# Lightning attention and a tanh-shrink layer on one core: q and k tiles read as runs of 224 numbers

## The chip, the cores and the metric

The kernel runs on one core of a Trainium2 chip. The core has a matrix engine (PE, with PEld for its weight loads), a vector engine (DVE), ScalarE (ACT), GpSimd (POOL), which here only issues transfers, and SyncE (SP), which issues transfers too. Sixteen DMA engines move the data of all queues. The metric is the device time of one execution in microseconds (us); lower is better.

## What is computed

The input is q, k and v of shape (4, 8, 768, 64) (batch, head, token, head size), a decay lam for each head, and two weight matrices. A decaying linear attention is followed by a two-layer network without bias; all arithmetic is in 32-bit floats (the weights come as 64-bit floats and are rounded on the chip).

```python
for b in range(nb):                       # blocks of 64 tokens
    intra = einsum('bhic,bhjc->bhij', qb, kb) * Dmask
    intra = einsum('bhij,bhjd->bhid', intra, vb)
    inter = einsum('bhid,bhde->bhie', qb * lam_pow, kv_state)
    out[:, :, sl] = intra + inter
    kv_state = lam_block * kv_state + einsum('bhsd,bhse->bhde', kb * rev_pow, vb)
x = out.transpose(0, 2, 1, 3).reshape(3072, 512)
h = x @ w_in                              # 512 x 2048
return (h - tanh(h)) @ w_out              # 2048 x 512
```

## The kernel before

The 768 tokens are cut into six groups of 128 (g = 0 to 5); a group has the four batches, so 512 rows go through the network together. The two matrix products are computed with fewer multiplications, by sums and differences of quarter blocks (seven products in place of eight, for some of them twice nested), so the vector engine adds and subtracts a great deal beside PE. The factors of the weights are made once, written to scratch memory (`factors`, `fine`, `fine_in`), and streamed back from there into a ring of eight tiles `wb` of 256 KB by POOL's queue, one after the other as PE frees them.

Attention needs q and k with the head size on the partitions. For groups 0 and 1, PE transposes natural tiles. For groups 2 to 5 SP loads q and k a second way (`load_blocks`, L143 to L152): a tile `blk` of 128 partitions by 4 by 128 numbers. Partitions 32c to 32c + 31 hold a quarter of a pair of heads (c // 2 chooses the head, c % 2 the half of the head size), and each line of 32 numbers is one token's half. A tile takes 16 transfers, each of 128 runs of 32 numbers (128 bytes). VectorE then transposes each 32 by 32 square (`STREAM_TRANSPOSE`, L335) into qt or kt, one instruction of 512 numbers a partition for each, and multiplies qt by the decay into qd (L346). There are 4 groups x 4 batches x 2 = 32 such tiles; they come from a pool of seven (`late["blk"]`, L1098).

The order of SP's transfers is written out by hand in `load` (L154 to L186), and every transfer of it is kept in program order: for a group, q and k of batches 0, 1, 2, then q of batch 3, natural k and v of batches 0 and 1, k of batch 3, natural k and v of batches 2 and 3 (for group 2 the natural tiles of batches 0 to 2 come first). A transfer waits for the one eight before it on the queue and, if its tile was used before, for the transposes that read the tile. What waits holds up all that is behind it on SP.

Attention of a group is done in pieces during the network's work on the group before it: transposes, scores (PE L362, masked on DVE at L367), state (PE L437, DVE L441 and L443), old state times qd (PE L482), scores times v (PE L501). Batches 2 and 3 are transposed in the midst of the nested second product (`down_twice`, PE L908), batches 0 and 1 near its end and in the first product (`inner_steps`, PE L697, with L686, L688, L714 and L716 taking results from PE's banks). The transposes of DVE are kept in program order; the rest of DVE's order is put together by a scheduler. In `down_twice`, L914 subtracts one quarter from another, which PE's second zw step then reads. The natural k tiles are decayed on ScalarE (L404).

Of the kernel before, what the change touches and what calls it, by code (L numbers as in the profile page):

```python
# [9 lines left out]
F32 = mybir.dt.float32  # L10
# [8 lines left out]
BLK = 128  # L19
# [5 lines left out]
def kernel(  # L25
# [32 lines left out]
    nc = tc.nc  # L58
    B, H, S, D = q.shape
    NTOK, DM = out.shape  # L60
    DFF = moe_w_in.shape[1]
    NP = H // 2
# [62 lines left out]
    def tied(yes, op):  # L125
        return tc.keep_in_program_order(op) if yes else op


    raw, late = {}, {}
    chunks = [(g, b) for g in range(NG) for b in range(B)]  # L130
    at = {"loaded": 0}

# [10 lines left out]
    def load_blocks(g, b, names):  # L143
        for name, src in (("q", q), ("k", k)):
            if name in names:
                x = late["blk"].tile([128, NP, BLK // 32, 32], F32, name=f"{name}_blk", tag="blk")
                for p in range(NP):
                    for c in range(4):
                        blk = src[b, 2 * p + c // 2, ts(g, BLK), ts(c % 2, 32)]
                        tc.keep_in_program_order(  # L150
                            nc.sync.dma_start(out=x[ts(c, 32), p], in_=blk.rearrange("(r t) a -> t r a", t=32)))  # L151
                raw[g, b][name + "b"] = x  # L152

    def load(n):  # L154

        while at["loaded"] < min(n, len(chunks)):
            g, b = chunks[at["loaded"]]
            if g < GB:  # L160
                raw[g, b] = {}
                load_natural(g, b, "qk")
                for x in (b - 1, b) if b % 2 else ():
                    load_natural(g, x, "v")
                at["loaded"] += 1
                continue
            for b in range(B):
                raw[g, b] = {}
            nat = "kv"

            first = (0, 1, 2) if g == GB else ()
            for b in first:
                load_natural(g, b, nat)
            for b in range(B - 1):
                load_blocks(g, b, "qk")
            load_blocks(g, 3, "q")
            for b in (0, 1):
                if b not in first:
                    load_natural(g, b, nat)
            load_blocks(g, 3, "k")  # L180
            for b in (2, 3):
                if b not in first:
                    load_natural(g, b, nat)
            at["loaded"] += B
# [113 lines left out]
    def bank(name, tag, bufs):  # L298
        return psum.tile([128, 512], F32, name=name, tag=tag, bufs=bufs)
# [27 lines left out]
    def att_transpose(g, bs):  # L327
        for b in bs:
            load(g * B + b + 1)
            t = raw[g, b]  # L330
            qt = work.tile([128, NP, BLK], F32, name="qt", tag="qt")
            kt = work.tile([128, NP, BLK], F32, name="kt", tag="kt")
            for dst, x in ((qt, "q"), (kt, "k")):
                if g >= GB:
                    tc.keep_in_program_order(nc.vector.transpose(out=dst.rearrange("d p i -> d (p i)"),  # L335
                                                                 in_=t[x + "b"].rearrange("d p r a -> d (p r a)")))
                else:
                    tp = bank("tp", "att", 4).rearrange("d (p s) -> d p s", p=NP)
                    for p in range(NP):
                        tied(g == 0 or p == 0, nc.tensor.transpose(out=tp[:, p, :], in_=t[x][:, 2 * p:2 * p + 2, :],  # L340
                                                                   identity=ident))
                    tied(g == 0, nc.scalar.activation(dst, tp, AF.Copy))
            qd = None
            if g > 0:
                qd = work.tile([128, NP, BLK], F32, name="qd", tag="qd")
                nc.vector.tensor_tensor(  # L346
                    qd.rearrange("d p (a i) -> d p a i", a=2), qt.rearrange("d p (a i) -> d p a i", a=2),
                    fwd[:, :, None, :].to_broadcast([128, NP, 2, HALF]), op=AL.mult)
            tr[g, b] = (qt, kt, qd)
            if g == 1:  # L350
                att_decay(g, b)
# [37 lines left out]
    def att_decay(g, b):  # L389
        kp = raw[g, b]["k"].rearrange("s (p j) d -> s p j d", j=2)  # L390
        if g > 0:
            nc.vector.tensor_tensor(kp, kp, bwd, op=AL.mult)
            return
        for j in range(2):
            tc.keep_in_program_order(nc.vector.tensor_tensor(
                kp[:, :, j, :], kp[:, :, j, :], whole[j][:, :, BLK - 1:BLK].to_broadcast([128, NP, D]), op=AL.mult))
# [122 lines left out]
    def attention(g):  # L519
        pieces = [[(fn, g, bs) for fn in (att_transpose, att_scores, att_state, att_inter, att_intra)] for bs in ((0, 1), (2, 3))]  # L520
        pieces[1].append((att_sums, g, None))
        return pieces
# [504 lines left out]
    for b in (0, 1):  # L1027
        att_transpose(0, (b,))
        att_decay(0, b)
        att_scores(0, (b,))  # L1030
    att_state(0, (0, 1))
    half = up_plain(0, (11, 21))
    att_transpose(0, (2,))
    att_decay(0, 2)
    weights(1)
# [59 lines left out]
            sums_in((1, 4, 6).index(kt))  # L1095
    first_results()
    early.close()
    late["blk"] = ctx.enter_context(tc.tile_pool(name="blk", bufs=2 * B - 1))  # L1098
    late["pool"] = ctx.enter_context(tc.tile_pool(name="late", bufs=1))


# [165 lines left out]
```

## Time and profile before

| | us |
|---|---|
| three runs | 651.76, 652.22, 656.49 |
| median | 652.22 |
| the profiled execution | 656.83 |
| its span, first to last instruction | 655.1 |

The page's other lines of interest, as shares of the span: the queue of POOL's transfers took 50.4% of the sixteen DMA engines' time for 104.62 MB in 31,792 packets, SP's queue 26.3% for 34.12 MB in 136,224 packets. Where the document shows the order of time of an engine, the columns are start, duration, engine, line, operation, what it writes and reads, and in brackets how long the engine stood idle before it and what released it. In the view of waits, the columns are the total, the number of times and the longest. A group of instructions shows total and mean duration (us, then ns), then the idle time before it.

From the same profiled execution: SP issues a `blk` transfer in 0.43 us (median) and a tile's 16 in 7.6 to 14.8 us; q tiles are transposed in 693 to 712 ns, k tiles in 661 to 714 ns.

### The profile page before, as it was taken

What the parts mean: (1) busy time and instruction counts of PE and PEld (TensorE: products, weight loads), DVE (VectorE), ACT (ScalarE), POOL (GpSimd) and SP (SyncE); (2) the same over time, 40 slices, a digit from 0 to 9 for tenths busy, and PEclk for the clock granted to TensorE, in tenths of its full rate; (3) what the DMA queues carried; (4) which work ended last, traced back from release to release, by engine and by line L of the source; (5) the groups of instructions that cost most, each with busy time, mean ns of one, the idle gap of its engine ahead of it and who ended that gap; (6) DMA issues with size and microseconds to landing.
All of it is one profiled execution on the core that took longest, in us unless ns stands there. A gap on an engine that the chain in (4) does not pass through costs nothing.

```text
span 655.1 us, 16636 instructions
## 1 busy us (share of the span) xinstructions
PE 638.0 (97%) x6440; PEld 586.0 (89%) x6440; DVE 478.5 (73%) x948; ACT 267.5 (41%) x620; POOL 228.4 (35%) x397
## 2 busy tenths in 40 slices
PE   7899999999999999799999999999899999999998
PEld 6788878888888999798899998899898899998997
DVE  4577697776798875669966679988567987467953
ACT  4799585403431422245241246333335342333310
POOL 0000345745533453410355530254320245521251
PEclk9999999999999999899999999999999999999999
DMA  9999998968765998785799985698883377742394
GB/s 212 219 247 237 284 274 295 322 181 244 230 166 140 266 289 235 210 192 121 195 243 275 303 226 153 156 277 247 263 179 99 104 244 226 246 126 68 90 305 150
DMA packets 168238, 139.80 MB, mean 213 GB/s; under 512 B 136864, under 2 KB 138016, under 8 KB 168160
## 3 DMA queue, kind: packets, MB, share of 16 engines
q0 software_dynamic: 31792, 104.62, 50.4%
q1 hardware_dynamic: 136224, 34.12, 26.3%
q8 instruction: 51, 0.84, 0.5%
q14 instruction: 27, 0.22, 0.1%
q10 hardware_dynamic: 144, 0.00, 0.0%
HBM read 111.94 MB, written 26.74 MB: 212 GB/s over the span
## 4 chain that ended last, share of the span: by engine, by line
PE 78%; DVE 8%; DMA 7%; SPq 3%; ACT 2%; issue 1%; DVEq 0%; ACTq 0%
PE y L697 9%; PE plain L851 9%; PE y L908 9%; PE acc L995 7%; PE h L966 7%; PE zw L908 7%; PE z L697 5%; PE y L554 4%; PE y L619 3%; PE zs L619 3%; DMA k_blk<-in_k_dram 3%; PE w L697 2%; PE z L554 2%; SPq L151 2%; DMA q_blk<-in_q_dram 2%; PE op L501 2%
## 5 line engine op out<-in xcount | busy, mean ns | idle before, releaser
L795 POOL DMA_DIRECT2D wb<-fine x133 | 71.6, 539 | 158.8 <-PE plain L851 107.9
L851 PE MATMUL plain<-wb,g 128*128 128x256 f32 x416 | 96.0, 381 | 0.0
L851 PEld LDWEIGHTS plain<-wb,g 128*128 128x128 f32 x416 | 77.5, 190 | 10.4
L966 PE MATMUL h<-xt,w 128*128 128x256 f32 x256 | 57.9, 382 | 1.8 <-DVE w L296 1.8
L798 POOL DMA_DIRECT2D wb<-factors x64 | 34.5, 539 | 70.3 <-PE z L697 47.9
L966 PEld LDWEIGHTS h<-xt,w 128*128 128x128 f32 x256 | 47.7, 190 | 9.0 <-DVE w L296 2.0
L912 ACT ACTIVATE q<-y 128x128 f32<-128x128 f32 x76 | 21.1, 278 | 79.9 <-PE y L908 78.7
L908 PE MATMUL y<-wb,g 128*128 128x128 f32 x336 | 44.8, 278 | 0.0
L688 ACT ACTIVATE g<-y 128x512 f32<-128x512 f32 x24 | 14.3, 597 | 71.5 <-PE y L697 71.5
L792 POOL DMA_DIRECT2D wb<-fine_in x60 | 32.5, 543 | 28.7 <-PE z L697 11.9
L600 ACT ACTIVATE th<-g 128x512 f32<-128x512 f32 x48 | 29.5, 627 | 30.2 <-DVE g L625 30.1
L908 PEld LDWEIGHTS y<-wb,g 128*128 128x128 f32 x336 | 40.7, 192 | 0.7
L404 ACT ACTIVATE k_nat<-k_nat,mask 128x64 f32<-128x64 f32 (+1 forms) x128 | 35.0, 335 | 1.1 <-DMA k_nat<-in_k_dram 1.1
L697 PE MATMUL z<-tt,wb 128*128 128x128 f32 x256 | 32.7, 280 | 0.0
L995 PE MATMUL acc<-wt,g 128*128 128x256 f32 x144 | 32.7, 380 | 0.0
L601 DVE TENSOR_TENSOR g<-g,th 128x512 f32<-128x512 f32 x48 | 32.0, 684 | 0.4
L697 PEld LDWEIGHTS z<-tt,wb 128*128 128x128 f32 x256 | 31.1, 196 | 0.0
L995 PEld LDWEIGHTS acc<-wt,g 128*128 128x128 f32 x144 | 27.3, 190 | 3.7
L619 PE MATMUL y<-xt,w 128*128 128x256 f32 x128 | 30.3, 379 | 0.0
L619 PE MATMUL zs<-xt,ws 128*128 128x256 f32 x128 | 30.2, 379 | 0.0
L908 PE MATMUL zw<-wb,g 128*128 128x128 f32 x224 | 30.2, 278 | 0.0
L292 ACT ACTIVATE r<-raw 128x512 int16<-128x512 uint32 x32 | 25.0, 782 | 7.9 <-DMA raw<-in_moe_w_out_dram 3.5
(233 smaller groups left out, 1475.8 us busy)
## 6 DMA issues: line engine op xcount, KB each, us to landing
wb<-fine POOLq DMA_DIRECT2D x133, 256.0 KB, 3.9
wb<-factors POOLq DMA_DIRECT2D x64, 256.0 KB, 4.5
wb<-fine_in POOLq DMA_DIRECT2D x60, 256.0 KB, 5.1
v_nat<-in_v_dram SPq DMA_DIRECT2D x24, 256.0 KB, 5.2
raw<-in_moe_w_out_dram POOLq DMA_DIRECT2D x12, 512.0 KB, 6.1
k_nat<-in_k_dram SPq DMA_DIRECT2D x20, 256.0 KB, 4.9
fine<-wt POOLq DMA_DIRECT2D x17, 256.0 KB, 3.7
raw<-in_moe_w_in_dram SPq DMA_DIRECT2D x8, 512.0 KB, 6.0
```

The source lines that it names most:

```text
L404: tc.keep_in_program_order(nc.scalar.activation(k_h, k_h, AF.Copy, scale=mask[0:rows, h % 2, h // 2, HALF - 1:HALF]))
L554: nc.tensor.matmul(out=t[:, m, :], lhsT=wt[:, kt, ts(m, 128)], rhs=x[:, kt, :], start=first and m == 0 and kt == 0, stop=kt == 1, skip_gro ...
L601: nc.vector.tensor_tensor(dst(c), src, th, op=AL.subtract)
L619: nc.tensor.matmul(out=t[:, m, :], lhsT=wt[:, kt, ts(m, 128)], rhs=x[:, kt, :], start=False, stop=kt == 1, skip_group_check=True)
L697: nc.tensor.matmul(out=dst[:, ts(u, 128)], lhsT=a, rhs=b, start=(x in (1, 5) or x == 2 and not filled) and u == 0, stop=True, skip_group_c ...
L792: nc.gpsimd.dma_start(out=t.rearrange("p m c -> p (m c)"), in_=fine_in[INNER.index(n_[1]), (5, 6, 3).index(x_)].rearrange("p u c -> p (u c)"))
L795: nc.gpsimd.dma_start(out=t.rearrange("p m c -> p (m c)"), in_=fine[TWICE.index(n_), SUB.index(x_)].rearrange("p u c -> p (u c)"))
L798: nc.gpsimd.dma_start(out=t, in_=factors[XAT[FACT[n_][1]]][:, 2 * x_:2 * x_ + 2, :])
L851: tied(held["yes"], nc.tensor.matmul(out=t[:, m, :], lhsT=a[:, u, kt, ts(m, 128)], rhs=wb[:, kt, :], start=first and u == 0 and m == 0 and ...
L908: tied(held["yes"], nc.tensor.matmul(out=dst, lhsT=a[:, u, :], rhs=wb[:, ts(u, 128)], start=x in (1, 2) and u == 0, stop=u == NU - 1, skip ...
L966: tied(u == 0 or held["yes"], nc.tensor.matmul(out=hm[c][:, m, :], lhsT=w1[u][:, i, a, ts(m, 128)], rhs=xt[0, t][:, i, :], start=m == 0 an ...
L995: tied(held["yes"], nc.tensor.matmul(out=acc[n][:, r, :], lhsT=a[:, ts(r, 128)], rhs=b, start=kt == 0 and r == 0, stop=kt == KH - 1, skip_ ...
```

## The change

A tile is read in four transfers, one for each quarter c. The 128 tokens of a head are 32 stretches of four tokens (4 x 64 = 256 numbers), one to a partition. Of each stretch a run of 224 numbers is read, from its start (c % 2 = 0) or from its 33rd number (c % 2 = 1), so that of its seven lines of 32 numbers those at 0, 2, 4 and 6 are the wanted halves of four tokens; the other three are read and not used. A tile grows from 2,048 to 3,584 bytes a partition, and the pool from which it comes shrinks from seven tiles to four. Since a partition now holds tokens 4t to 4t + 3 where it held t, t + 32, t + 64 and t + 96, the transposes read every second line and write token 4t + r: neighbouring numbers of a written line lie four apart.

```diff
+    RUN = 4 * D - 32
@@ load_blocks
-                x = late["blk"].tile([128, NP, BLK // 32, 32], F32, name=f"{name}_blk", tag="blk")
-                for p in range(NP):
-                    for c in range(4):
-                        blk = src[b, 2 * p + c // 2, ts(g, BLK), ts(c % 2, 32)]
-                        tc.keep_in_program_order(
-                            nc.sync.dma_start(out=x[ts(c, 32), p], in_=blk.rearrange("(r t) a -> t r a", t=32)))
-                raw[g, b][name + "b"] = x
+                x = late["blk"].tile([128, NP, RUN], F32, name=f"{name}_blk", tag="blk")
+                heads = src[b].rearrange("(p j) s d -> j p (s d)", j=2)
+                for c in range(4):
+                    runs = heads[c // 2, :, g * BLK * D:(g + 1) * BLK * D].rearrange("p (t x) -> t p x", t=32)
+                    tc.keep_in_program_order(nc.sync.dma_start(
+                        out=x[ts(c, 32)], in_=runs[:, :, c % 2 * 32:c % 2 * 32 + RUN]))
+                raw[g, b][name + "b"] = x.rearrange("d p (r a) -> d p r a", a=32)[:, :, ::2]
@@ att_transpose
-                    tc.keep_in_program_order(nc.vector.transpose(out=dst.rearrange("d p i -> d (p i)"),
-                                                                 in_=t[x + "b"].rearrange("d p r a -> d (p r a)")))
+                    tc.keep_in_program_order(nc.vector.transpose(
+                        out=dst.rearrange("d p (t r) -> d p r t", r=4), in_=t[x + "b"]))
@@
-    late["blk"] = ctx.enter_context(tc.tile_pool(name="blk", bufs=2 * B - 1))
+    late["blk"] = ctx.enter_context(tc.tile_pool(name="blk", bufs=B))
```

The order in which the engines get their instructions is the same in both kernels on PE, ScalarE and POOL. On SP only the number of transfers to a tile differs. On DVE two transposes of k move ahead, so that each now follows the transpose of q before it: that of group 2, batch 3 past seven instructions, and that of group 3, batch 0 past sixteen.

## The prediction

> **What bounds the kernel now.** I read the page first, then the waits of PE, then the order of time of DVE and PE around the one long wait, then the same orders around the vector engine's transposes. All times are of the profiled execution: 656.83 us, of which the span is 655.1 and 1.73 lies around it. The three runs shown are 651.76, 652.22 and 656.49.
>
> ```profile
> PE 638.0 (97%) x6440; PEld 586.0 (89%) x6440; DVE 478.5 (73%) x948; ACT 267.5 (41%) x620; POOL 228.4 (35%) x397
> ```
>
> PE is busy 97% of the span, so an edit off PE can give back only what PE waits: 17.1 us, of which the waits with a named cause make 14. The largest is one wait of 3.4 us, and it hangs on this change:
>
> ```profile
> PE y L697 <- DVE g L686: 3.4, 1, 3.4
> ```
> ```profile
> 253.46 0.70 DVE L335 STREAM_TRANSPOSE qt<-q_blk 128x512 f32<-128x512 f32 x1
> 260.05 0.71 DVE L335 STREAM_TRANSPOSE kt<-k_blk 128x512 f32<-128x512 f32 x1 [5.89 <-DMA q_blk<-in_q_dram]
> ...
> 265.57 0.68 DVE L686 TENSOR_TENSOR r<-g,z 128x512 f32<-128x512 f32 x1
> 266.17 0.68 DVE L686 TENSOR_TENSOR g<-g,y 128x512 f32<-128x512 f32 x1
> ```
> ```profile
> 262.42 1.06 PE L697 MATMUL y<-tt,ws 128*128 128x128 f32 x8
> 266.90 1.34 PE L697 MATMUL y<-xt,w 128*128 128x128 f32 x8 [3.42 <-DVE g L686]
> 268.04 1.92 PE L697 MATMUL z<-tt,wb 128*128 128x128 f32 x8
> 269.75 1.73 PE L697 MATMUL z<-xt,wb 128*128 128x128 f32 x8
> ```
> ```profile
> 264.00:267.00 3.00, 0.10 (x1) 0.10 (x1) 2.93 (x6) 0.00 (x0) 3.00 (x7) 1.00 0.70 161
> 267.00:270.00 3.00, 3.00 (x18) 3.00 (x19) 1.74 (x4) 0.00 (x0) 1.07 (x3) 0.62 1.04 326
> 270.00:273.00 3.00, 3.00 (x24) 3.00 (x23) 1.37 (x2) 0.60 (x1) 1.08 (x2) 0.81 0.96 322
> ```
>
> DVE stands 5.89 us before kt of group 3, batch 1, because SP gets that tile's 16 issues out only from 247.11 to 257.80 (each waits for the transfer eight before it). DVE comes late to L686, and PE stands 3.42 us. The third view is stretches of time; the third number from the end is PE's granted clock, 0.62 and 0.81 after the gap. So the 24 matmuls from 266.90 to 271.31 take 4.41 us, where three sets of eight at 0.89 us (their spacing before the gap) take 2.67. The stall costs 3.42 + 1.74 = 5.16 us. 656.83 - 5.16 = 651.67, which is where two of the three runs lie; I read these as executions in which that tile came in time.
>
> **The change part by part.**
>
> *SP issues.* 32 tiles lose 12 of 16 issues. A tile's 16 took 7.6 to 14.8 us on SP; four at the median 0.43 us take 1.7. PE, ACT and POOL keep their instruction order; SP's order of tiles stays too.
>
> *Bytes.* A tile grows from 2048 runs of 128 bytes (256 KB) to 512 of 896 (448 KB). From 425 to 447 us SP's queue moves only such tiles: 5413 packets, 19.3% of 16 engines in 22 us, so 12.5 ns a packet; with 16 small packets for each transfer a tile costs 2304 x 12.5 / 16 = 1.8 us of all engines. The weights' queue there moved 5.25 MB in 71.1%, 48 ns for 1000 bytes, so an 896-byte run costs between 43 and 43 + 12.5 = 55 ns: 512 of them are 1.4 to 1.8 us. An equal or lower load, but in larger bursts (up to eight transfers of 112 KB under way where eight of 16 KB were).
>
> *Four tiles in the ring instead of seven.* The pool stays at 14,336 bytes a partition. Tiles q2, k2, q3, k3 of a group (q and k of batches 2 and 3) now wait for the transposes of batches 0 and 1, and the next group's first four for those of batches 2 and 3. Queued behind on SP are the natural k and v. Place by place: group 2's second half is released at 190 to 193 and needed at 211.6; group 4's first half at 326.3 to 329.4, needed at 355.96 and 361.84; group 5's at 428.3 to 431.4, needed at 454.77 and 466.25; group 3's natural k follows the transpose of 253.5 instead of being issued at 288. All have ten us or more, so I take nothing. One place is tight, group 3's batch 0 (the second rival).
>
> *DVE's order.* Two transposes move: kt of group 2, batch 3 past 7 instructions, and kt of group 3, batch 0 past 16, to the place beside its qt. The second now stands ahead of the two ss of L367, the state of L443 and L914.
>
> *The stall at 253 to 271.* Group 3's batch 1 is released at about 217 and needed at 253.5. I take the stall as gone: -5.16. What is late next there is PE's own z, which ends at 258.85.
>
> *The transposes' writes.* 32 transposes now write each number 16 bytes from the one before. The trace has no vector instruction with such a step.
>
> ```profile
> L335 DVE STREAM_TRANSPOSE qt<-q_blk 128x512 f32<-128x512 f32 x16 | 11.3, 704 | 1.9 <-DMA k_blk<-in_k_dram 1.9
> ```
>
> Lower bound: 0. Between: ScalarE's copy that reads 32-bit numbers at a step of two and writes 16-bit numbers at a step of two (L292) takes 782 ns against 597 for a dense one, a factor 1.31, which on 0.69 us is +0.21. Upper: vector instructions of 128 and 512 numbers take 283 and 685 ns, 1.05 ns a number; if every write takes a second slot, 512 x 1.05 = +0.54 us a transpose. I take the upper value: the ScalarE row still writes four numbers into each stretch of 16 bytes and reads two from one, and lost 31%; the transposes will write one, so they lie beyond that row, on the upper end's side. What that costs is read from the places where DVE has no room before PE:
>
> ```profile
> 328.75 0.67 DVE L335 STREAM_TRANSPOSE kt<-k_blk 128x512 f32<-128x512 f32 x1
> 329.35 0.65 DVE L346 TENSOR_TENSOR qd<-qt,fwd 128x512 f32<-128x512 f32 x1
> 329.92 0.68 DVE L914 TENSOR_TENSOR gS<-gS,s 128x512 f32<-128x512 f32 x1
> ```
> ```profile
> 329.69 1.06 PE L908 MATMUL y<-wb,gS 128*128 128x128 f32 x8
> 330.65 1.16 PE L908 MATMUL zw<-wb,gS 128*128 128x128 f32 x8
> ```
>
> After PE's zw ends, DVE does two adds, four transposes with two qd, then L914 ending at 330.60, and PE's next zw, which reads that gS, starts at 330.65. No slack: four slower transposes put 4 x 0.54 = 2.14 us on PE. The same sequence stands at 428.30 (L914 at 431.89, zw at 432.62) and 530.29 (533.88, 534.61): 3 x 2.14 = 6.43. In group 2's second half L914 ends at 221.48 and PE's zw starts at 222.26; less 0.05 for the handing over the slack is 0.73: 2.14 - 0.73 = 1.41. At 190 the four have 197.45 - 194.29 = 3.2 us before PE's z: nothing. The pairs at 355.96, 361.84, 454.77 and 466.25 add 1.07 each and meet DVE idle of 2.19 (at 367.4) and 1.70 (at 460.2): nothing. Sum +7.84. These gaps are 2.1 us each; after PE's 1.68 us gap at 464 the clock stayed 1.00, so I add no slow clock.
>
> The Trainium skill ("SBUF — State Buffer", Door 1) says that memory works in lines of 16 bytes, that full rate needs at least two accesses to a line, and that each access that crosses to a new line pays; it gives no price. By that sentence this step is the first that loses, as in the sum; by its list of how far one can stride for free (4 numbers of 32 bits) it could still be free, which is the first rival. No row of this trace decides between them.
>
> *The wait at 464* (1.68 us, a store that took 6.37 us to land among q and k tiles): bursts may lengthen or shorten it, between -1.7 and +2; I take 0, as there is as much to move.
>
> Sum: 656.83 - 5.16 + 7.84 = **659.5 us**, +0.4% on the profiled execution and +1.1% on the median.
>
> **The rivals.**
>
> *The step is free (not slower).* Decided by the transposes' mean: at 0.70 us only the stall's end remains, 651.7 us, -0.1% on the median (654.3 with +0.21 a transpose: 3 x 0.84 + 0.11). For it: the input stays in runs of 32 numbers, and no vector row shows that a step costs anything. Against: the ScalarE row. Below it lies only the 1.68 us of 464: 650.
>
> *The burst comes late (slower still).* Group 3's k0 goes out at 214.7 to 216.4, after kt of group 2, batch 2, and must land by 225.5. The two 256 KB loads that SP issued at 207.7 and 208.1 took 6.3 and 9.5 us to land, so 512 KB took 9.9 us from the first issue. If 6.3 holds for k0, it lands at 222.7; q0 and k0 together are 896 KB, which from 213.0 at that pace end at 230.4, 4.9 us too late. I took the first, since those loads move 256-byte runs. DVE would stand at kt, and L914 behind it (ended 230.69, PE's zw at 230.74, no slack) would pass it on: 664.4, and 666.1 if the clock falls again for 1.74. For it: the DMA share of 215 to 260 is 0.93.
>
> *More than two slots a write*, four say: 1.61 more a transpose, 3 x 6.43 + 5.7 = 25; 676.7.
>
> *Faster by over 1%* would need under 645.7, which no row supports.
>
> **How the numbers follow.** 0.50 for the forecast, 0.27 for a free or nearly free step, 0.15 for the late burst on top, 0.05 for more slots, 0.03 for something faster. The range runs from the free step to the late burst: 651 to 667. About 1% of the median, 645.7 to 658.7, is what a measurement can tell. The forecast lies 0.8 above that bound: of its 0.50 I count 0.34 slower; with 0.13 of the burst and 0.05 of more slots 0.52 slower, 0.45 the same, 0.03 faster. The likeliest case alone: 657 to 662.
>
> **What would show it.** Right: transposes of about 1.24 us; no DVE wait on q or k tiles near 250; PE waits of about 2 us on DVE's L914 (L915 then) at three places and a shorter one near 222; no clock dip near 267. Wrong: transposes near 0.70; a DVE wait before kt near 225; waits of PE on wb, which would mean that the weights' stream lost to the bursts.

## The result and the profile after

The changed kernel takes 671.52 us (median of 668.88, 675.73, 670.97 and 672.07) beside 652.66 for the kernel before in the same comparison: a ratio of 1.0283 [1.0216, 1.0351]. The prediction was 659.5 us with a range up to 667: slower was right, the size was not. A second comparison (e8 below) gave 1.0265 [1.0214, 1.0315]. The ratios leave out a run that took over 1.5% more than the fastest of its kernel; among all runs here that is one, in e9.

The profiled execution took 668.88 us, 667.1 of it the span. PE has hardly more to do, 641.1 us of work beside 638.0:

```profile
PE 641.1 (96%) x6440; PEld 588.0 (88%) x6440; DVE 490.3 (73%) x948; ACT 267.8 (40%) x620; POOL 228.3 (34%) x397
```

So most of the time went into PE's waits and the slow clock behind some of them. PE's waits of the changed kernel (one line has been added above these places, so L914 is L915 now, and so on):

```profile
PE zw L909 <- DVE gS L915: 4.5, 4, 1.2
PE z L698 <- ACT r L689: 3.6, 1, 3.6
PE op L502 <- issue: 2.9, 1, 2.9
PE y L909 <- DMA wb<-fine: 2.0, 2, 1.3
PE kv L438 <- issue: 2.0, 1, 2.0
```

Only the first line was in the sum. It is the transposes' step. The same place on DVE and on PE as was shown of before, around 328:

```profile
326.48 1.09 DVE L336 STREAM_TRANSPOSE qt<-q_blk 128x512 f32<-128x512 f32 x1
327.39 1.11 DVE L336 STREAM_TRANSPOSE kt<-k_blk 128x512 f32<-128x512 f32 x1
328.34 0.69 DVE L347 TENSOR_TENSOR qd<-qt,fwd 128x512 f32<-128x512 f32 x1
328.93 0.69 DVE L915 TENSOR_TENSOR gS<-gS,s 128x512 f32<-128x512 f32 x1
```
```profile
327.38 1.06 PE L909 MATMUL y<-wb,gS 128*128 128x128 f32 x8
329.67 1.16 PE L909 MATMUL zw<-wb,gS 128*128 128x128 f32 x8 [1.23 <-DVE gS L915]
```

A transpose takes 1.1 us instead of 0.7, L915 ends at 329.62, and PE's zw, which was ready at 328.44, starts at 329.67.

The two waits on "issue" are the surprise. PE stops in the middle of one group of like matmuls, released by no engine and no transfer that it waits for:

```profile
226.19 0.74 PE L438 MATMUL kv<-v_nat,k_nat 64*64 64x64 f32 x34
228.90 0.69 PE L438 MATMUL kv<-v_nat,k_nat 64*64 64x64 f32 x30 [1.96 <-issue]
...
448.30 1.16 PE L502 MATMUL op<-ss,v_nat 64*64 64x64 f32 x58
452.34 0.34 PE L502 MATMUL op<-ss,v_nat 64*64 64x64 f32 x6 [2.88 <-issue]
452.61 1.59 PE L909 MATMUL zw<-wb,g 128*128 128x128 f32 x8
453.99 1.91 PE L909 MATMUL y<-wb,s 128*128 128x128 f32 x8
```

What PE lacks there is its own program. The page lists a queue 8 of kind "instruction": 51 packets of 16 KB, 0.84 MB in both kernels. For PE's 6440 matmuls and 6440 weight loads that is 65 bytes each, and the packets come faster where PE's matmuls do, one to some 128 of them: I read it as the queue that feeds PE. PE's records bear that out. Counted over its matmuls, weight loads and waits, PE stands still behind the 4034th instruction and behind the 9154th. That is 5120 instructions and 20 packets apart, 256 instructions of 64 bytes to a packet. With a boundary at every 256 instructions, none of 600 crossings in the twelve executions traced comes less than 1.29 us after the end of its packet. The kernel before crosses the second place 1.46 us after the packet's end: it has hardly any time to spare there.

The two packets before these gaps were under way on their DMA engine from 226.47 to 227.61 and from 449.74 to 450.85; PE went on 1.29 and 1.49 us after their ends. They took no longer than elsewhere (1.14 and 1.11 us; the median of all 51 is 1.07, and 1.05 before). They began late: the first when PE had begun 188 matmuls from the 1792nd on (78 in the kernel before), the second 162 from the 4352nd on (72 before).

What else used the DMA engines then, by stretches of time (duration, busy time of PE, PEld, DVE, ACT and POOL, PE's clock, DMA share, GB/s), first before, then after:

```profile
222.00:225.00 3.00, 3.00 (x76) 2.88 (x79) 1.36 (x4) 1.98 (x9) 1.93 (x4) 1.00 1.01 308
225.00:229.00 4.00, 4.00 (x110) 3.93 (x102) 2.72 (x5) 0.75 (x3) 1.07 (x3) 1.00 0.77 210
```
```profile
225.00:229.00 4.00, 2.04 (x105) 1.78 (x107) 3.40 (x5) 1.23 (x5) 0.76 (x2) 1.00 1.07 302
448.00:452.00 4.00, 1.45 (x61) 1.12 (x59) 0.48 (x1) 1.18 (x5) 0.54 (x1) 1.00 1.04 318
452.00:455.00 3.00, 2.66 (x19) 2.60 (x20) 1.46 (x3) 0.66 (x2) 0.51 (x1) 0.69 0.33 109
```

All sixteen engines are full during both gaps. That alone makes no gap: the kernel before has them as full from 222 to 225 (1.01), and its PE is busy throughout. Within the gaps POOL's queue took 79% and 88% of the engines' time, SP's 24% and 13%; what differs is how much SP had put on the engines before, as the table further down counts. SP issued q and k tiles at 213 to 231 and at 430 to 444 with nothing between them, up to eight transfers of 112 KB under way at once. The last row shows the clock after the second gap: 24 matmuls from 452.61 take 4.41 us, 1.73 more than at their usual spacing.

The other two waits have the same burst beside them. PE waits 1.29 and 0.75 us for weights (wb). And at 474 ScalarE's r waits for a store that POOL issued at 465.17 and that landed after 8.3 us (6.3 before); behind that PE starts at 474.18 after 3.60 us (1.68 before), and the slow clock costs 1.46 more.

The difference of the two profiled executions can be put together. Before without its stall is 655.1 - 5.16 = 649.94 us of span. To this come 4.52 (step), 6.57 (the two fetch gaps and 1.73 of slow clock), 2.04 (wb), 3.38 (the store: 3.60 - 1.68 + 1.46) and 0.64 (a wait of z on L704 at 248.78): 667.1. That it closes to the tenth is partly luck: the other waits of PE are about 1.6 us shorter in the changed kernel, its other busy time about 1.6 us longer, and neither is in the sum. So by this reading 4.5 us belong to the step and 12 to 13 to the bursts. The experiments test that.

### The profile page after: what moved, and what is told of

It reads as the page before. It is cut to its first block, busy times and chain, and to the rows that moved or that the text cites. A ratio compares the mean times of both kernels' runs of the same rounds, so it can differ in the third digit from the quotient of the medians.

```text
span 667.1 us, 16191 instructions
## 1 busy us (share of the span) xinstructions
PE 641.1 (96%) x6440; PEld 588.0 (88%) x6440; DVE 490.3 (73%) x948; ACT 267.8 (40%) x620; POOL 228.3 (34%) x397
## 4 chain that ended last, share of the span: by engine, by line
PE 57%; issue 19%; DMA 7%; POOL 7%; DVE 6%; ACT 2%; SPq 1%; POOLq 0%; DVEq 0%; ACTq 0%
PE plain L852 8%; PE acc L996 7%; PE h L967 7%; PE y L698 6%; PE y L909 6%; PE zw L909 5%; PE z L698 4%; POOL wb L796 3%; DMA wb<-fine 3%; PE y L620 2%; PE zs L620 2%; POOL wb L799 2%; PE w L698 1%; PE y L555 1%; DMA out_dram<-q 1%
## 5 line engine op out<-in xcount | busy, mean ns | idle before, releaser
L852 PE MATMUL plain<-wb,g 128*128 128x256 f32 x416 | 96.1, 381 | 0.0
L852 PEld LDWEIGHTS plain<-wb,g 128*128 128x128 f32 x416 | 77.5, 190 | 10.5
```

The source lines that it names most:

```text
L852: tied(held["yes"], nc.tensor.matmul(out=t[:, m, :], lhsT=a[:, u, kt, ts(m, 128)], rhs=wb[:, kt, :], start=first and u == 0 and m == 0 and ...
```

## The experiments

In the first four expectations, A is the theory that the bursts cost the most, in its form A1 through the bytes that SP has under way at once; B is the theory that the transposes' step does.

**The step with small transfers (e1_step).** The kernel before, 16 transfers of 128-byte runs and seven tiles, but with four neighbouring tokens to a partition, so that the transposes write at a step of four.

```diff
-  ... in_=blk.rearrange("(r t) a -> t r a", t=32)
+  ... in_=blk.rearrange("(t r) a -> t r a", t=32)
-  nc.vector.transpose(out=dst.rearrange("d p i -> d (p i)"), in_=t[x + "b"].rearrange("d p r a -> d (p r a)"))
+  nc.vector.transpose(out=dst.rearrange("d p (t r) -> d p r t", r=4), in_=t[x + "b"])
```

> The tiles are loaded as before (16 transfers of 128-byte runs, seven tiles), only with four neighbouring tokens to a partition, so that the transposes write at a step of four. Theory A (the step is only a part: transposes start 0.31 us later each, four places, 4.5 us; the rest of the loss is what the large transfers do to the other queues): 4.5 us above the kernel before, 656 to 658; PE waits on gS at four places of about 0.9 and three times 1.2 us, none for issue, none on wb. Theory B (the step is all of the loss): about 671, ratio 1.028.

Measured: 684.55 us, 1.0452 [1.0396, 1.0508], slower than the change itself. It doesn't isolate the step. With the source in this order SP needed 0.60 us for an issue instead of 0.43, so a tile's sixteen came later; DVE stood 7.0, 6.8, 4.8 and 4.2 us before transposes of q and k, and PE's longest wait on gS was 7.5 us. Neither theory's time came. PE had no fetch gap and no wait on wb. The step had to be tried another way (e6_step_only).

**The bursts without the step (e2_runs).** The changed kernel with its loads and its ring, but the transposes write densely. The tokens of q and k in groups 2 to 5 then stand in another order, so these scores are not the reference's; the work is the same.

```diff
-  out=dst.rearrange("d p (t r) -> d p r t", r=4), in_=t[x + "b"]
+  out=dst.rearrange("d p (r t) -> d p r t", r=4), in_=t[x + "b"]
```

> The tiles are loaded as in the changed kernel (four transfers of 896-byte runs, four tiles), but the transposes write densely as before; so q and k of groups 2 to 5 stand in another order of tokens, and the output is not the reference's. Theory A: the changed kernel less 4.5 us, about 666, with PE's waits for issue (2 to 5 us), on wb (about 2) and on the store before L689 (3 to 4) still there and no waits on gS over 0.3. Theory B: the time of the kernel before, 652.

Measured: 1.0239 [1.0177, 1.0302], 664.5 us of span. PE's waits:

```profile
PE y L909 <- DMA wb<-fine: 3.9, 4, 1.3
PE z L698 <- ACT r L689: 3.4, 1, 3.4
PE op L502 <- issue: 2.7, 1, 2.7
...
PE kv L438 <- issue: 0.9, 1, 0.9
```

The transposes are back at 0.70 us, the waits on gS are gone, and most of the loss is still there. B falls. The waits on wb are longer than in the changed kernel: where DVE no longer holds PE up, the weights do.

**Smaller and more transfers (e3_eight, e4_sixteen).** The changed kernel, with the same runs of 896 bytes, the same bytes and the same step, cut into eight transfers of 56 KB a tile or sixteen of 28 KB. Since a transfer waits for the one eight before it, this halves or quarters what is under way.

```diff
-  nc.sync.dma_start(out=x[ts(c, 32)], in_=runs[:, :, c % 2 * 32:c % 2 * 32 + RUN])
+  for p in (0, 2):          # e4: for p in range(NP), one p at a time
+      nc.sync.dma_start(out=x[ts(c, 32), p:p + 2], in_=runs[:, p:p + 2, c % 2 * 32:c % 2 * 32 + RUN])
```

> The changed kernel with eight transfers of 56 KB a tile for four of 112 KB: the same runs, bytes, ring and writes, but half as much under way, since a transfer waits for the one eight before it. Theory A1 (depth: what counts is how much of SP's data stands in the engines' queues ahead of PE's instructions, the weights and the store): PE's waits for issue and on wb together fall from 6.9 us to 3 or less, total about 662 to 665. Theory A2 (the bytes or the 896-byte runs themselves): the waits stay within 1.5 us of 6.9, total 668 to 674. A third, that tiles then come late and DVE stands at kt of group 3, would show as DVE waits on k tiles near 225.

> The same with sixteen transfers of 28 KB a tile: a quarter as much under way. Theory A1: no waits for issue or on wb over 0.5 us, the store before L689 lands in 6 us or less; but SP again needs 7 to 10 us a tile, which with four tiles makes DVE stand at the transposes of k of group 3, batches 0 and 1, 5 us or more together. Total 658 to 668 by how late those are. Theory A2: waits for issue and on wb stay at 5 to 7 us on top of that, 672 or more.

Measured: 666.39 us, 1.0161 [1.0112, 1.0209], and 680.8 us, 1.0378 [1.033, 1.0425]. Waits with eight, then with sixteen:

```profile
PE zw L910 <- DVE g L916: 5.1, 1, 5.1
PE zw L910 <- DVE gS L916: 4.3, 4, 1.3
PE z L699 <- ACT r L690: 2.5, 1, 2.5
PE op L503 <- issue: 2.0, 1, 2.0
DVE kt L337 <- DMA q_blk<-in_q_dram: 5.1, 1, 5.1
```
```profile
PE zw L910 <- DVE gS L916: 13.7, 4, 9.9
PE y L699 <- DVE g L688: 8.8, 3, 5.4
```

The burst's waits shrink: issue and wb together 6.88 us in the changed kernel, 2.0 with eight, 0.4 with sixteen, where also the waits on ScalarE's r are down to 1.3. What returns in their place is lateness. With eight, k of group 3, batch 0 is 5.1 us late; with sixteen, DVE waits 28 us in all before transposes of q and k, and the sum is worse than the change. So both times missed what A1 expected (662 to 665, and 658 to 668). As to the waits the depth theory stands, and the two harms trade against each other.

**Runs of two tokens (e5_two).** Runs of 96 numbers (384 bytes), eight transfers of 48 KB, four tiles; the transposes write at a step of two.

```diff
+  RUN = 2 * D - 32
+  ... eight transfers: c in range(4), r in range(2), in_=runs[:, :, c % 2 * 32:c % 2 * 32 + RUN]
+  nc.vector.transpose(out=dst.rearrange("d p (r t s) -> d (p r) s t", r=2, s=2), in_=t[x + "b"])
```

> Runs of 96 numbers (two tokens, 384 bytes), eight transfers of 48 KB a tile, four tiles, and the transposes write at a step of two numbers. Theory 'bytes under way': eight transfers are 384 KB against the changed kernel's 896 KB (and 448 KB in the run with eight transfers of 56 KB, which left PE 2.0 us of fetch gaps and no wait on wb); so fetch gaps and waits on wb together stay under 2.5 us. Tiles come no later than in that run (same number of issues, less to move): waits on q and k tiles of VectorE up to 5 us. Step: if every second write shares its 16 bytes, the transposes take between 0.70 and 0.90 us and their sites cost PE under 2 us. Time 655 to 664. Rival 'the step is what costs, whatever its size': transposes at 1.1 us, waits on gS 4 to 5 us, 660 to 668.

Measured: 1.0042 [1.0011, 1.0073]. The transposes' groups:

```profile
L338 DVE STREAM_TRANSPOSE qt<-q_blk 128x512 f32<-128x512 f32 x16 | 11.3, 708 | 0.0
L338 DVE STREAM_TRANSPOSE kt<-k_blk 128x512 f32<-128x512 f32 x16 | 10.9, 683 | 0.0
```

708 and 683 ns, where before had 704 and 675: a step of two costs nothing, and no tile is late (0.0 idle). With PE's fetch gap at 1.1 us, wb at 1.1 and the store's wait at 2.8 (1.7 before), and without the stall of the kernel before, this is nearly its time.

**The step alone (e6_step_only).** The kernel before with its loads, tiles and orders, only that the transposes write at a step of four; tokens of q and k in groups 2 to 5 stand in another order, so these scores are not the reference's.

```diff
+  nc.vector.transpose(out=dst.rearrange("d p (t r) -> d p r t", r=4), in_=t[x + "b"])
```

> The kernel before, its loads and orders untouched, but the transposes write at a step of four numbers, as in the change; the tokens of q and k in groups 2 to 5 then stand in another order, so the output is not the reference's. This is the step alone. Theory 'the step costs PE 1.23 us at each of three or four sites': transposes at 1.07 to 1.13 us, PE waits on L914's gS 3.7 to 4.9 us in all, no fetch gaps, no waits on wb; the one wait of the kernel before on a late k tile stays where it was; ratio to before 1.003 to 1.009, 654 to 662 us beside a before of 652 to 656. Rival 'the step slows VectorE enough to make the whole +2.8%': ratio 1.02 or more.

Measured: 1.005 [1.0025, 1.0075], and

```profile
L335 DVE STREAM_TRANSPOSE qt<-q_blk 128x512 f32<-128x512 f32 x16 | 17.7, 1108 | 0.6 <-DMA k_blk<-in_k_dram 0.6
```
```profile
PE zw L908 <- DVE gS L914: 4.3, 4, 1.3
...
PE y L697 <- DVE g L686: 2.6, 1, 2.6
...
PE z L697 <- ACT r L688: 1.2, 1, 1.2
```

The step costs what the changed kernel's trace says, 4.3 us of PE's waits at four places; by the ratio, 3.3 us in all. Within the intervals the two parts multiply to the whole: 1.0239 x 1.0050 = 1.029, where the changed kernel has 1.0283 and 1.0265.

**The changed kernel once more (e8_after_again).**

> The changed kernel once more, on the same chip as the three runs beside it. The theory of the bursts: ratio 1.022 to 1.035 as in the first comparison, fetch gaps of PE (idle in the middle of a group, released by nothing) 3 to 6 us and waits on wb 1 to 4 us, at places that differ from the first execution. Rival 'the first execution was an odd one': ratio under 1.015 and fetch gaps under 1 us.

Measured: 1.0265 [1.0214, 1.0315]. The fetch gaps are at the same two places, the first of them longer, and a short third one (L852) has come:

```profile
PE kv L438 <- issue: 3.4, 1, 3.4
PE op L502 <- issue: 3.1, 1, 3.1
...
PE y L909 <- DMA wb<-fine: 1.4, 1, 1.4
...
PE plain L852 <- issue: 0.8, 1, 0.8
```

I had expected other places, but the two main ones did not move. PE stops behind the same instructions as in the first execution, here 34 matmuls into the same group of 64:

```profile
227.24 0.74 PE L438 MATMUL kv<-v_nat,k_nat 64*64 64x64 f32 x34
231.34 0.69 PE L438 MATMUL kv<-v_nat,k_nat 64*64 64x64 f32 x30 [3.36 <-issue]
```

Both places lie among matmuls of 64 x 64, which use up the program fast (64 of them in 1.1 us).

**Half as much under way (e9_spaced).** e3 and e5 change the size of a transfer and the bytes under way together. Here the transfers stay at 112 KB, each followed by one of a single number to a place that nothing reads, so that of the eight that may be under way four are large.

```diff
   nc.sync.dma_start(out=x[ts(c, 32)], in_=runs[:, :, c % 2 * 32:c % 2 * 32 + RUN])
+  nc.sync.dma_start(out=small[n:n + 1], in_=src[b, c, g * BLK, 0:1])
```

> The changed kernel, its four transfers of 112 KB a tile untouched, each followed on SP by a transfer of one number to a place nobody reads: of the eight that may be under way at most four are then large, 448 KB. Theory 'bytes under way': as in the run with eight transfers of 56 KB (also 448 KB): idle in the middle of a group 1 to 3 us, nearly no wait on wb, the fetch near 222 us begins with PE about 80 to 110 matmuls into it (before 78, changed 188 and 202); the tiles come somewhat later, so one DVE wait of about 5 us on group 3's batch 0; ratio 1.012 to 1.020. Rival 'the size of one transfer (112 KB in one piece ahead of everything else) does the harm, not how many are queued': fetch gaps of 4 us and more, waits on wb of 2 us, ratio 1.022 or more.

Measured: 1.0139 [1.0088, 1.0191] from the runs of 662.48, 663.77 and 669.90 us; with the fourth, 675.24 us, it would be near 1.018. The profiled one, 661.9 us of span:

```profile
PE z L702 <- ACT r L693: 2.0, 1, 2.0
...
PE z L702 <- DMA wb<-fine_in: 1.2, 1, 1.2
PE op L506 <- issue: 1.0, 1, 1.0
PE zw L913 <- DMA wb<-fine: 0.6, 1, 0.6
PE op L487 <- issue: 0.5, 1, 0.5
```

Adding transfers made the changed kernel faster, 5 to 7 us of fetch gaps became 1.5, and the store's wait went from 3.6 to 2.0. The fetch near 222 began at 79 matmuls, as foretold. The rival (the size of one transfer) falls. Another is not separated: every kernel here with less under way also takes more issues for a tile, so SP hands out its data at a slower pace. Two things I expected didn't come: the waits on wb are still 1.8 us, so for the weights this run does not show that the bytes under way decide; and no tile was late.

Over all runs the delay of the fetch grows with the bytes under way. The table is worked out from the records of queue 8 and of PE's matmuls in each trace: how long after the earliest of eleven executions (all but e1's), at the same count of matmuls, the 15th and the 35th packet began, and the gap that followed. The second column counts SP's q and k tiles alone.

| kernel | most under way, KB | 15th late, us | gap near 230 | 35th late, us | gap near 450 |
|---|---|---|---|---|---|
| before | 8 x 16 = 128 | 0.4 | 0 | 0.4 | 0 |
| step only | 128 | 0.3 | 0 | 0.3 | 0 |
| sixteen | 8 x 28 = 224 | 1.1 | 0 | 0.3 | 0 |
| two tokens | 8 x 48 = 384 | 0.6 | 0 | 1.6 | 1.05 |
| eight | 8 x 56 = 448 | 1.0 | 0 | 2.7 | 2.04 |
| spaced | 4 x 112 = 448 | 0.5 | 0 | 1.5 | 1.01 |
| runs, dense | 8 x 112 = 896 | 6.0 | 0.91 | 3.4 | 2.74 |
| changed | 896 | 5.8 | 1.96 | 3.5 | 2.88 |
| changed again | 896 | 8.1 | 3.36 | 3.6 | 3.06 |

Up to 448 KB the 15th packet shows no order, 0.3 to 1.1 us; at 896 KB it is 5.8 to 8.1. By the issues and landings, SP had 96 KB under way when that packet fell due in the kernel before, 336 with eight and with the spaced transfers, 784 to 896 in the last three rows. POOL's weights do not explain the difference: five of them, 1280 KB, were under way then with eight, spaced and changed alike.

In each case with a gap PE goes on 1.3 to 1.6 us after the packet's end. A run of 896 bytes takes an engine 60.5 ns on average in the changed kernel; spread evenly, eight transfers of 112 KB are 64 runs on each engine, 3.9 us. That is near the delays of 3.4 to 3.6, as if the fetch waited for all that was queued on its engine before it; the 5.8 to 8.1 are more than one filling of the queue. The Trainium skill ("DMA: Bandwidth & Descriptors", section "Queues, rings and completion order") says that an engine goes round the queues that have work and takes one packet of typically 9 to 17 descriptors from each. By that rule SP's queue alone would hold a fetch up by some 0.5 to 1.0 us, an estimate at 60.5 ns a run, however much it has under way; the spaced run against the changed one, 0.5 beside 5.8 us, shows that it does not stay the same. Which of the chip's queues the fetch really stands behind, no run here shows.

**A better order for the kernel before (e7_later, e10_latest).** The stall of 5.16 us in the kernel before can go without touching a load, if DVE's two transposes for group 3, batch 1 stand behind what PE needs first.

```diff
-  run(early_pieces)                               # at (4, 1)
+  if g > 1:
+      run(early_pieces)
...
   if g < GI and (kind, x) == (4, 5):
       every(factors_twice(2))
+      run(early_pieces)                           # e7; in e10 for g == 1 after (4, 6)
```

> The kernel before with VectorE's two transposes of group 3, batch 1 placed later, behind the four L781 of the factors of group 2 and behind L686's r, so that a k tile landing at 260 holds up nothing that PE waits for. Theory: PE's wait of 3.42 us on L686 and the 1.74 us of slow clock behind it go, and the next late thing is PE's own z: 651 to 653 where before has 655 to 657 in such an execution, ratio 0.993 to 1.0. Rival: the transposes now stand ahead of something else that PE waits for (L914 of group 3's first half), and the time is the same or up to 3 us more.

> The kernel before with VectorE's transposes of group 3, batch 1 placed later still, behind all three L686 that PE waits for there (the run with them behind the first L686 left PE a wait of 1.57 us). Theory: no PE wait on L686 near 264, no slow clock, and nothing else waits for these transposes before their scores: 649 to 652 in executions where before has 652 to 657, ratio 0.988 to 0.998. Rival: the tiles that wait for these two places of the ring come later and another wait of 2 to 5 us appears after 280: 652 to 657.

Measured: 652.69 us for e7, 0.9971 [0.9938, 1.0005], a gain that can't be told from none. The k tile still came late (its transpose starts at 263.62, after a wait of 2.64 us), and one L686 was behind it:

```profile
PE y L697 <- DVE g L686: 1.6, 1, 1.6
```

e10: 652.34 us beside 656.18, 0.9942 [0.9917, 0.9967], by its ratio the fastest kernel of this study, a small gain but clear of the interval. Its PE runs through here, and the transposes follow at 273.8 without a wait before them:

```profile
264.27 1.06 PE L697 MATMUL y<-xt,w 128*128 128x128 f32 x8
265.17 1.06 PE L697 MATMUL z<-tt,wb 128*128 128x128 f32 x8
266.06 1.06 PE L697 MATMUL z<-xt,wb 128*128 128x128 f32 x8
```
```profile
273.78 0.70 DVE L335 STREAM_TRANSPOSE qt<-q_blk 128x512 f32<-128x512 f32 x1
274.41 0.67 DVE L335 STREAM_TRANSPOSE kt<-k_blk 128x512 f32<-128x512 f32 x1
```

Its median is 0.3 above the 649 to 652 that I had expected. The tiles behind these two did not come late enough to hold PE up, so that rival falls.

## Why the prediction was right or wrong

**The stall at 253 to 271: right.** The changed kernel's transposes there follow each other without a wait:

```profile
257.58 1.09 DVE L336 STREAM_TRANSPOSE qt<-q_blk 128x512 f32<-128x512 f32 x1
258.52 1.09 DVE L336 STREAM_TRANSPOSE kt<-k_blk 128x512 f32<-128x512 f32 x1
```

e10, which has no such stall, is 0.6% or 3.8 us faster over many executions, a little less than the 5.16 of the profiled one (and its wait on L688 near 460 is shorter too, 0.83 us).

**SP's issues, the ring of four, DVE's moved transposes: right.** The changed kernel has no wait on a q or k tile above 0.6 us. The late burst at group 3's k0 did not come; it came with eight issues a tile (5.1 us in e3), so the place was tight as described, but four issues are quick enough.

**The transposes' step: right mechanism and places, too large a size.** Foretold were three gaps of 2.14 us and one of 1.41, 7.84 in all; measured were 1.23, 1.22, 1.22 and 0.85, 4.52. A transpose takes 1.10 us, 0.40 more, not 0.54; and the next instruction starts before it ends, so from start to start it is only 0.31 more (0.94 beside 0.63). The argument that chose the upper end, ScalarE's 31% at a step of two, was a poor guide: VectorE loses nothing at a step of two (e5). The Trainium skill's sentence ("SBUF — State Buffer", Door 1) that a line of 16 bytes needs two accesses for full rate agrees with this: two writes to a line at 708 ns, one write at 1108. Its list, which would let 32-bit numbers stride by 4 for free, does not: by that the step would have cost nothing.

**Bytes: here the prediction failed.** The step that priced them, "An equal or lower load, but in larger bursts", put nothing into the sum. The load was in fact a little higher: an 896-byte run took 60.5 ns, not 43 to 55, so a tile costs 512 x 60.5 / 16 = 1.94 us of all engines where 2048 x 12.9 / 16 = 1.65 were needed before. That is not what cost 2%. It is the second half of the sentence, left without a price: seven times as much was under way at once, and three others on the same engines came later, PE's instructions (6.57 us with the slow clock), the weights (2.04) and the store (3.38). The weights stood in the list of what would prove it wrong, without a chance; the instruction fetch was not thought of, though the page of before lists its queue.

**The wait at 464: its range was right in sign only.** "I take 0, as there is as much to move" became 1.92 more, at the upper bound of +2, and 1.46 of slow clock behind it, for which the prediction had no term.

**The result's side** was right for half the reason: without the bursts the change would, by e6, stand near +0.5% or below (e6 kept the stall that the change removes; a version with the step, the early tiles and no bursts was not tried). With them it is past the range.

## What to carry to other kernels

Larger transfers are no gain in themselves on a queue whose depth is counted in transfers, as SP's is here (eight): the depth in bytes grows with them, and whatever else needs the DMA engines at short notice, the matrix engine's own program included, can come later for it. When a change merges transfers, multiply size by depth before and after, and look in the trace for what else is small and urgent. A group of like matmuls that stops in the middle with no releaser is to be checked against the instruction queue before any theory on the engines.

## What the runs showed of the hardware that was not expected

- PE's instruction fetch competes with data. With 896 KB under way on SP's queue its packets began 3.4 to 8.1 us late at the two places followed here, and PE stood 0.9 to 3.4 us in the middle of a group; with 128 to 224 KB there was no such gap.
- VectorE's 32-bit transposes write at a step of two for free (708 and 683 ns) and at a step of four in 1.10 us.
- SP's issue of the same 16 KB took 0.60 us instead of 0.43 when only the order in which the source's runs go to the partitions was changed (e1).
- The length of a gap alone does not decide whether PE's clock falls. After 2.50 us (e3) it was 0.50, after 3.36 us (the changed kernel again) and 2.59 us (e6) it stayed at 1.00. In each trace the granted clock changes only on a grid of 3.41 us. Over the twelve executions, wherever PE was idle for 2.27 us or more of one such stretch at full clock, the next stretch had 0.50, and nowhere after 1.97 us or less; the grid cut the gap of 3.36 us into 1.97 and 1.39. The Trainium skill ("TensorE: Matmul & The Clock Gate", Part 1) gives a window of 3.4 us that runs freely, without regard to the kernel. The grid agrees with it, and the falls show that less than a whole window of idle time is enough.
